# A transformer-like kernel on one core: layer-norm outputs of eleven token tiles transposed by VectorE and DMAs through DRAM in place of TensorE

## Chip, core and metric

The kernel runs on one core of one Trainium2 chip. The metric is the device time of one execution in microseconds. Before the change the median of three runs is 756.94 us (755.6 to 759.04).

## What is computed

Two layers, each a linear-attention block and an expert-lookup block, on 2048 tokens of 576 numbers, all float32:

```python
x = x + A(layernorm(x));  x = x + B(layernorm(x));  x = x + A(layernorm(x));  x = x + B(layernorm(x))

def A(x):                                   # H = 32 heads of 18
    q, k, v = heads(x @ wqkv)
    pq, pk = phi(q), phi(k)                 # phi(t) = where(t > 0, t + 1, exp(t)) + 1e-6
    kv = einsum("bhsd,bhse->bhde", pk, v);  z = einsum("bhsd->bhd", pk)
    o = einsum("bhqd,bhde->bhqe", pq, kv) / (einsum("bhqd,bhd->bhq", pq, z)[..., None] + 1e-6)
    return merged(o) @ wo
```

B scores every token against two sets of eight keys per head, takes the best pair, and adds a gated row of `v` for it. The change lies in the first A block alone.

## The kernel before

The 2048 tokens are cut into 16 tiles of 128. In the first layer, for each tile t, the layer-norm output `y` (128 tokens on the partitions, 576 features along the row, stored as 640 with 64 features doubled) must be turned so that features lie on the partitions; it is then the stationary side of the products with `wqkv`. To keep float32 accuracy a product is made of three passes: each operand is held as a rounded part `hi` and a rest `lo`, so `product` (L205) issues 28 matmuls for one 128 x 576 result.

One tile's way through the first layer's front:

- `first_load` (L587) loads the x tile. `first_ln` (L592): `statistics` (L156) on VectorE (two `BN_STATS`, one `BN_AGGR`, "stf", "mvf") and GpSimd ("rsf"), then `normalized` (L183) on ScalarE writes `y` ("yf", L187).
- `front_T` (L231) calls `transposed` (L190): five TensorE transposes into a PSUM tile "ptf" (L197), then `split` (L100): ScalarE copies to "thif" (L102), VectorE subtracts to "tlof" (L103).
- `front_k` (L234), `front_v` (L239), `front_q` (L250): the products "ppk", "ppv", "ppq" (L212). `phi` (L216) of k and q is one Exp on ScalarE (L218) and two VectorE passes (L219, L221; "ek", "eq"). phi of q goes to DRAM ("pq_d", L254).
- `front_state` (L275): five matmuls add the tile's part of kv into the PSUM tile "kva".

The loop at L724 runs t = 2 to 12. Round t computes k, v, q and the state of tile t, and the layer norm and transposes of tile t + 1. In between it also prepares the second block's weights: while t is at most 9 a round loads eight pieces of `wq_t` ("fold", L540, 288 KB each) and multiplies them at its end (`fold_mm`, L542, "fold_ps"); rounds 4, 6, 8 and 10 also move a finished chunk out (`fold_out`, L553, three ScalarE copies "foldf") and transpose it (`fold_T`, L561: five TensorE transposes "fold_pt", then copies and subtractions "shi" and "slo").

Within a round TensorE runs k, v, q, the transposes of tile t + 1, the state, the fold matmuls. In rounds 10 to 12 the transposes stand ahead of q. The block is inside `in_order` (L142), which ties TensorE, ScalarE, VectorE and GpSimd to the order in which the code issues. SP, which issues all DMAs, isn't tied; its order is the scheduler's, and a DMA that waits on SP holds up those behind it. PSUM has four tiles in rotation: one is "kva" throughout, one "fold_ps" while it fills; the rest serve k, v, q and the transposes. Behind the loop, a long order written out by hand (L752) starts with k and q of tile 13.

Of the kernel before, what the change touches and what calls it, by code (L numbers as in the profile page):

```python
# [11 lines left out]
F32 = mybir.dt.float32  # L12
F32R = mybir.dt.float32r
BF16 = mybir.dt.bfloat16
I32 = mybir.dt.int32
AF = mybir.ActivationFunctionType
ALU = mybir.AluOpType
# [5 lines left out]
P = 128  # L23
NT = S // P
# [11 lines left out]
NB = 5  # L36
# [21 lines left out]
def network(ctx, tc, x_in, wqkv, wo, wq_t, k_t, u_t, v2, c_mask, c_mask4, c_ident, c_code, c_code1, c_scale, c_shift, out):  # L58
    nc = tc.nc

    cp = ctx.enter_context(tc.tile_pool(name="cp", bufs=1))
    wk = ctx.enter_context(tc.tile_pool(name="wk", bufs=2))
    ps = ctx.enter_context(tc.tile_pool(name="ps", bufs=4, space=PSUM))
    dr = ctx.enter_context(tc.tile_pool(name="dr", bufs=1, space=DRAM))

    def psum(name):
        return ps.tile([P, 1024], F32, tag="ps", name=name)
# [28 lines left out]
    hl_d = [dr.tile([P, 2, NB, P], F32, name=f"hl_d{t}") for t in range(NT)]  # L96
    pq_d = [[dr.tile([P, D], F32, name=f"pq_d{l}_{t}") for t in range(NT)] for l in range(2)]
    x_d = [dr.tile([P, D], F32, name=f"x_d{t}") for t in range(NT)]

    def split(src, hi, lo, eng=nc.vector):  # L100

        nc.scalar.activation(hi, src, AF.Copy)  # L102
        eng.tensor_tensor(lo, src, hi.bitcast(F32), op=ALU.subtract)  # L103
# [29 lines left out]
    def split_weight(tiles, c0, hi, lo, rem, which=range(NB), eng=nc.vector):  # L133
        for b in which:
            cols = slice(c0, c0 + D)
            if b != rem:
                split(tiles[b], hi[:, b, cols], lo[:, blocks(rem)[b][1], cols], eng)
            else:
                split_mixed(tiles[b], hi[:, b, cols])

    @contextmanager
    def in_order(*engines):  # L142

        ins = nc.cur_bb.bb.instructions
        last = ins[-1]
        yield
        ins = nc.cur_bb.bb.instructions
        start = next(i for i in reversed(range(len(ins))) if ins[i] is last) + 1
        for e in engines:
            mine = [i for i in ins[start:] if i.engine == e]  # L150
            for x, y in zip(mine, mine[1:]):
                tc.add_manual_dep(y, x.name, mybir.DependencyInfo(mybir.DependencyClass.NoSync, mybir.DependencyReason.DATA),
                                  reason="in_order")
# [28 lines left out]

    def normalized(xt, rs, n):  # L183

        y = wk.tile([P, 2, 320], F32, tag="y", name=f"y{n}", bufs=3)
        x2 = bass.AP(tensor=xt.tensor, offset=xt.offset, ap=[xt.ap[0], [256, 2], [1, 320]])
        nc.scalar.activation(y, x2, AF.Identity, scale=rs[:, 0:1], bias=rs[:, 1:2])  # L187
        return y.rearrange("p a b -> p (a b)")

    def transposed(y, n, more=None, tag="t", step=P):  # L190

        todo = [y[:, b * step:b * step + P] for b in range(NB)] if y is not None else []
        todo += [] if more is None else [more]
        w = len(todo) * P
        pt = psum(f"pt{n}")
        for b, x in enumerate(todo):
            nc.tensor.transpose(pt[:, b * P:(b + 1) * P], x, ident)  # L197
        nb = NB if tag == "t" else NB + 1
        hi = wk.tile([P, nb, P], F32R, tag=tag + "hi", name=f"thi{n}", bufs=4 if tag == "t" else 1)
        lo = wk.tile([P, nb, P], F32R, tag=tag + "lo", name=f"tlo{n}", bufs=4 if tag == "t" else 1)  # L200
        yield
        split(pt[:, :w], hi.rearrange("p a b -> p (a b)")[:, :w], lo.rearrange("p a b -> p (a b)")[:, :w])
        return hi, lo

    def product(tt, hi, lo, cols, n, cut=HALF, rem=REM, by_block=False):  # L205
# [18 lines left out]
    tt = {}  # L224
    xs = {}
    ys = {}
# [3 lines left out]

    def front_T(l, t):  # L231
        tt["f", l, t] = yield from transposed(ys.pop(("f", l, t)), f"f{l}_{t}")

    def front_k(l, t):  # L234
        k = product(tt["f", l, t], whi, wlo, D, f"k{l}_{t}", by_block=(l == 0 and t == 0))
        yield
        tt["fk", l, t] = phi(k, f"k{l}_{t}")
# [175 lines left out]
    def exp_T(l, t, c):  # L413

        y = ys.pop(("b", l, t)) if ok(t) else None
        cg = tt.pop(("cg", l, c)).rearrange("p a b -> p (a b)") if ok(c) else None
        if y is None and cg is None:
            return
        hi, lo = yield from transposed(y, f"b{l}_{t % 99}", cg, tag="t" if cg is None else "u")
        if y is not None:  # L420
            tt["b", l, t] = hi, lo
        if cg is not None:
            b = 0 if y is None else NB
            tt["c", l, c] = hi[:, b], lo[:, b]
# [127 lines left out]

    def fold_out(ch):  # L553
        p = fold_ps.pop(ch)
        f = wk.tile([P, 640], F32, tag="y", name=f"foldf{ch}", bufs=3)
        nc.scalar.activation(f[:, :320], p[:, :320], AF.Copy)
        nc.scalar.activation(f[:, 320:384], p[:, 256:320], AF.Copy)
        nc.scalar.activation(f[:, 384:], p[:, 512:768], AF.Copy)
        fold_st["f", ch] = f
# [21 lines left out]
    def warm_up(n):  # L581

        p = psum("warm")
        for i in range(n):
            nc.tensor.matmul(p[:, :512], junk[:, :P], junk[:, :512], start=True, stop=True)

    def first_load(l, t):  # L587
        xt = wk.tile([P, D], F32, tag="x", name=f"xf_{t}", bufs=3)
        nc.sync.dma_start(xt, x_in[t * P:(t + 1) * P, :])
        xs["f", t] = xt  # L590

    def first_ln(l, t):  # L592
        xt = xs.pop(("f", t))
        ys["f", 0, t] = normalized(xt, statistics(xt, f"f0_{t}"), f"f0_{t}")
# [43 lines left out]
    def ok(t):  # L638
        return 0 <= t < NT
# [3 lines left out]
    def run(l, *seq):  # L643


        for f, t, *n in seq:
            if f is bc or ok(t):
                g = begun.pop((f, l, t), None) or (exp_T(l, *t) if f is bc else f(l, t))
                for i in range(n[0] if n else 99):
                    if g is None or next(g, bc) is bc:  # L650
                        break
                else:
                    begun[f, l, t] = g
# [4 lines left out]
    k, v, q, fT, st = front_k, front_v, front_q, front_T, front_state  # L658
# [3 lines left out]
    L = NT - 1  # L662
# [30 lines left out]
    with in_order(*ALL):  # L693
        x0, x1 = xs.pop(("f", 0)), xs.pop(("f", 1))
        warm_up(14)
        rs0 = statistics(x0, "f0_0", soon=True)
        split_weight(wk_in, D, whi, wlo, REM, (0,))
        ys["f", 0, 0] = normalized(x0, rs0, "f0_0")
        split_weight(wk_in, D, whi, wlo, REM, (1, 2))
        run(0, (fT, 0, 1))  # L700
        warm_up(2)
        run(0, (fT, 0))
        split_weight(wk_in, D, whi, wlo, REM, (3,), nc.gpsimd)
        rs1 = statistics(x1, "f0_1", soon=True)
        split_weight(wk_in, D, whi, wlo, REM, (4,))
        ys["f", 0, 1] = normalized(x1, rs1, "f0_1")
        run(0, (k, 0, 1), (fT, 1))
        split_weight(wv_in, 2 * D, whi, wlo, REM, (0, 1))
        run(0, (k, 0), (k, 1, 1))
        split_weight(wv_in, 2 * D, whi, wlo, REM, (2, 3, 4))  # L710
        first_load(0, 2)
        wq_in = load_weight(wqkv, 0, REM, "w")
        small_loads()
        first_load(0, 3)
        run(0, (k, 1), (v, 0, 1))
        split_weight(wq_in, 0, whi, wlo, REM, (0, 1))
        run(0, (v, 0))
        first_ln(0, 2)
        split_weight(wq_in, 0, whi, wlo, REM, (2, 3))
        run(0, (v, 1, 1))  # L720
        split_weight(wq_in, 0, whi, wlo, REM, (4,))
        run(0, (st, 0), (fT, 2), (v, 1), (q, 0), (st, 1), (q, 1))
        PER, FIRST = 8, 13
        for t in range(2, FIRST):  # L724
            m0 = PER * (t - 2)
            groups = [m for m in range(m0, m0 + PER) if m < 2 * H]
            done = (m0 - 1) // 16 if m0 % 16 == 0 and 0 < m0 <= 2 * H else None
            for m in groups:
                fold_load(m)
            if t + 2 < NT:  # L730
                first_load(0, t + 2)
            if t + 1 < NT:
                first_ln(0, t + 1)
            run(0, (k, t, 1))
            if done is not None:
                fold_out(done)
            run(0, (k, t))
            run(0, (v, t, 1))
            if done is not None and groups:
                fold_T(done)  # L740
            run(0, (v, t))
            if groups:
                run(0, (q, t), (fT, t + 1), (st, t))
            elif t < L:
                run(0, (fT, t + 1), (q if t < L - 1 else st, t), (st if t < L - 1 else q, t if t < L - 1 else -1))
            if done is not None and not groups:
                fold_T(done)
            for m in groups:
                fold_mm(m)
# [101 lines left out]
```

## Time and profile before

| | us |
|---|---|
| median of three runs | 756.94 |
| lowest and highest | 755.6, 759.04 |
| span of the profiled execution (first to last instruction) | 753.7 |
| TensorE busy in it | 736.8 |
| VectorE busy | 456.8 |
| ScalarE busy | 289.1 |

The profiled execution is one run. The profiler gives its span; what lies around the span isn't in the trace, and the median stands 3.2 us above it. A timeline row reads: start, duration of the group, engine, line, operation, output <- inputs, shape, count, and in square brackets how long the engine stood idle before it and what ended that. Rows of consecutive equal instructions are merged. PE is TensorE's matmuls, PEld its weight loads, DVE VectorE, ACT ScalarE, POOL GpSimd, SPq the queue that issues DMAs. Matmuls are pipelined, so a group's duration reaches a little into the next one; the distance between two starts is the better measure.

### The profile page before, as it was taken

The page shows a single profiled execution, that of the slowest core. Times are in us where ns is not written, and L with a number is a line of the kernel's source. Part 1 is how long each engine was busy: PE and PEld are TensorE (multiplying, and loading weights), DVE is VectorE, ACT ScalarE, POOL GpSimd, SP SyncE. Part 2 cuts the span into 40 slices and gives each one's busy share as a digit, 9 for nine tenths or more (in the row PEclk, how much of TensorE's full clock was granted, in tenths as well). Part 3 has the DMA queues.
Part 4 walks back from the last instruction along what each step waited for, and adds up shares of the span by engine and source line. Part 5 has one row for each costly group of instructions (what it writes and reads, how often), then busy time and mean ns, then how long its engine had stood idle before and what let it go on. Part 6 is the DMA issues. An engine that isn't in the chain of part 4 may idle for free.

```text
span 753.7 us, 13987 instructions
## 1 busy us (share of the span) xinstructions
PE 736.8 (98%) x5356; PEld 693.2 (92%) x5356; DVE 456.8 (61%) x1008; ACT 289.1 (38%) x586; POOL 197.7 (26%) x540
## 2 busy tenths in 40 slices
PE   7999999999999999999999999999999999999996
PEld 5999989999998989999999999999999999999984
DVE  5532342324246887666666665563366789999996
ACT  5422232232333544444444443533234333343443
POOL 2110001000002543333333342230033343534331
PEclk9999999999999999999999999999999999999999
DMA  9736446631111322222232211321733213111201
GB/s 275 245 125 223 157 171 220 218 118 49 48 63 32 110 89 77 98 84 83 92 105 101 83 67 60 111 68 38 206 107 112 85 65 115 48 48 58 70 33 63
DMA packets 52267, 79.48 MB, mean 105 GB/s; under 512 B 5480, under 2 KB 22376, under 8 KB 52200
## 3 DMA queue, kind: packets, MB, share of 16 engines
q1 hardware_dynamic: 52200, 78.59, 31.8%
q8 instruction: 42, 0.69, 0.4%
q14 instruction: 25, 0.20, 0.1%
HBM read 55.01 MB, written 23.56 MB: 104 GB/s over the span
## 4 chain that ended last, share of the span: by engine, by line
PE 81%; DVE 10%; ACT 3%; issue 2%; POOL 2%; DMA 1%; SPq 0%; DVEq 0%; POOLq 0%; ACTq 0%
PE ppk L212 15%; PE ppv L212 15%; PE ppo L402 13%; PE pps L433 12%; PE ppq L212 11%; PE kva L283 4%; PE fold_ps L550 2%; PE ptf L197 2%; PE ptb L197 2%; PE po L517 2%; PE pto L197 2%; PE m L332 1%; DVE tloo L103 1%; DVE o L379 1%; DVE x L391 1%
## 5 line engine op out<-in xcount | busy, mean ns | idle before, releaser
L219 DVE TENSOR_SCALAR ek<-ek 128x576 f32<-128x576 f32 x32 | 14.7, 459 | 81.4 <-ACT ek L218 76.9
L212 PE MATMUL ppk<-whi,thif 128*128 128x288 f32 x320 | 50.4, 301 | 1.6 <-ACT thif L102 1.6
L402 PE MATMUL ppo<-ohi,thio 126*128 126x288 f32 (+1 forms) x320 | 50.9, 301 | 0.8 <-DVE ct L492 0.5
L212 PEld LDWEIGHTS ppk<-whi,thif 128*128 128x128 f32 x320 | 44.2, 188 | 5.6 <-issue 3.3
L163 POOL TENSOR_SCALAR rsf<-mvf 128x1 f32<-128x1 f32 x16 | 3.1, 192 | 175.6 <-DVE mvf L161 175.4
L212 PE MATMUL ppk<-whi,tlof 128*128 128x288 f32 x320 | 48.7, 296 | 0.3 <-DVE tlof L103 0.3
L212 PE MATMUL ppv<-whi,thif 128*128 128x252 f32 x320 | 48.0, 296 | 0.1
L187 ACT ACTIVATE yb<-x,rsb 128x640 f32<-128x640 f32 x32 | 29.5, 923 | 47.9 <-POOL rsb L180 47.9
L212 PE MATMUL ppv<-whi,tlof 128*128 128x252 f32 x320 | 47.6, 295 | 0.0
L219 DVE TENSOR_SCALAR eq<-eq 128x576 f32<-128x576 f32 x32 | 15.8, 493 | 51.7 <-ACT eq L218 51.7
L433 PE MATMUL pps<-shi,thib 128*128 128x512 f32 x160 | 44.4, 407 | 2.0 <-ACT thib L102 2.0
L402 PEld LDWEIGHTS ppo<-ohi,thio 126*128 126x128 f32 (+1 forms) x320 | 44.6, 189 | 1.9 <-issue 0.7
L212 PEld LDWEIGHTS ppk<-whi,tlof 128*128 128x128 f32 x320 | 44.6, 188 | 0.5 <-DVE tlof L103 0.5
L212 PEld LDWEIGHTS ppv<-whi,tlof 128*128 128x128 f32 x320 | 44.6, 188 | 0.0
L212 PEld LDWEIGHTS ppv<-whi,thif 128*128 128x128 f32 x320 | 44.2, 188 | 0.3 <-ACT thif L102 0.3
L438 ACT ACTIVATE s<-pps 128x512 f32<-128x512 f32 x32 | 19.1, 596 | 61.4 <-PE pps L433 61.4
L433 PE MATMUL pps<-shi,tlob 128*128 128x512 f32 x160 | 42.5, 395 | 0.0
L103 DVE TENSOR_TENSOR tlof<-ptf,thif 128x640 fp32r<-128x640 f32 x32 | 26.2, 818 | 24.3 <-ACT thif L102 24.2
L402 PE MATMUL ppo<-ohi,tloo 126*128 126x288 f32 x256 | 40.3, 295 | 0.0
L402 PE MATMUL ppo<-olo,thio 126*128 126x288 f32 x256 | 40.3, 296 | 0.0
L212 PE MATMUL ppk<-wlo,thif 128*128 128x288 f32 x256 | 39.9, 296 | 0.0
L212 PE MATMUL ppq<-whi 128*128 128x288 f32 x260 | 39.6, 299 | 0.1
(156 smaller groups left out, 1778.6 us busy)
## 6 DMA issues: line engine op xcount, KB each, us to landing
fold<-in_wq_t SPq DMA_DIRECT2D x64, 288.0 KB, 4.8
whi<-hl_d SPq DMA_DIRECT2D x26, 320.0 KB, 3.5
pq_d<-eq SPq DMA_DIRECT2D x19, 288.0 KB
pq<-pq_d SPq DMA_DIRECT2D x19, 288.0 KB, 3.3
xf<-in_x SPq DMA_DIRECT2D x16, 288.0 KB, 4.7
x<-in_x SPq DMA_DIRECT2D x16, 288.0 KB, 2.8
x_d<-x SPq DMA_DIRECT2D x16, 288.0 KB, 3.1
x<-x_d SPq DMA_DIRECT2D x16, 288.0 KB, 2.6
```

The source lines that it names most:

```text
L103: eng.tensor_tensor(lo, src, hi.bitcast(F32), op=ALU.subtract)
L187: nc.scalar.activation(y, x2, AF.Identity, scale=rs[:, 0:1], bias=rs[:, 1:2])
L197: nc.tensor.transpose(pt[:, b * P:(b + 1) * P], x, ident)
L212: nc.tensor.matmul(o[:, at:at + c1 - c0], tt[a == "lo"][:, b, :], wb[:, cols + c0:cols + c1], start=(i == 0), stop=(i == len(todo) - 1))
L219: nc.vector.tensor_scalar(e, e, 1.0, EPS, op0=ALU.min, op1=ALU.add)
L283: nc.tensor.matmul(a[:w, c * HC:(c + 1) * HC], vt[:, c * w:(c + 1) * w], fk[:, c * HC:(c + 1) * HC], start=(t == 0 and c == 0), stop=(t == ...
L332: nc.tensor.matmul(m[:c, h * 512:h * 512 + HALF], kvb[:n, b * HC:b * HC + c], wob[l][b][:n, h * HALF:(h + 1) * HALF], start=True, stop=True)
L402: nc.tensor.matmul(p[:, h * 512:h * 512 + HALF], hl[a][:r, b], w[:r, h * HALF:(h + 1) * HALF], start=(i == 0), stop=(i == len(todo) - 1))
L433: nc.tensor.matmul(p[:, :512], hl[a == "lo"][:, b, :], shi[:, b] if w == "hi" else slo[:, blocks(REM)[b][1]], start=(i == 0), stop=(i == l ...
L438: nc.scalar.activation(s[:, NE:], p[:, :512], AF.Copy)
L517: nc.tensor.matmul(p[:, b * 512:b * 512 + HALF], c[i], vmix[:, b * HALF:(b + 1) * HALF], start=(i == 0 and not based), stop=(i == 1))
L550: nc.tensor.matmul(p[32 * j:32 * j + 32, at:at + c1 - c0], kpad[:, ch // 2, 24 - 8 * a:56 - 8 * a], st[:, c0:c1], start=(a == 0), stop=(a ...
```

## The change

In rounds 2 to 12, so for tiles 3 to 13, the transposes leave TensorE. `front_flip` for tile t + 1 stands behind phi of `k(t)`: VectorE transposes the 32 x 32 blocks of `y` within each group of 32 partitions (one instruction, output `q`), one DMA writes `q` (128 x 640, 320 KB) to a DRAM tile `t_d`, and four DMAs, 80 KB each in pieces of 160 numbers (640 bytes), bring it back into a tile `r`, so that each block lands on its right partitions. `front_flipped` takes the place of the transposes' copies: ScalarE copies `r` to "thif", VectorE subtracts to "tlof", now from SBUF and in runs of 32. The tag "y" grows from three buffers to four, since `q` and `r` share it. Rounds 10 to 12 keep their order (tile t + 1 ahead of q). Tiles 0 to 2, 14 and 15 and all later transposes stay on TensorE.

```diff
+    t_d = [dr.tile([P, NB * P], F32, name=f"t_d{t}") for t in range(NT)]
...
-        y = wk.tile([P, 2, 320], F32, tag="y", name=f"y{n}", bufs=3)
+        y = wk.tile([P, 2, 320], F32, tag="y", name=f"y{n}", bufs=4)
...
+    def flip(y, d, n):
+
+        q = wk.tile([P, NB * P], F32, tag="y", name=f"q{n}", bufs=4)
+        nc.vector.transpose(q.rearrange("p (q b c) -> p b q c", q=4, b=NB), y.rearrange("p (b q c) -> p b q c", b=NB, q=4))
+        nc.sync.dma_start(d, q)
+        r = wk.tile([P, NB * P], F32, tag="y", name=f"r{n}", bufs=4)
+        w = 32 * NB
+        for a in range(4):
+            nc.sync.dma_start(r[32 * a:32 * a + 32].rearrange("r (i e) -> r i e", i=4),
+                              d[:, a * w:(a + 1) * w].rearrange("(i r) e -> r i e", i=4))
+        return r
+
+    def flipped(r, n):
+
+        hi = wk.tile([P, NB, P], F32R, tag="thi", name=f"thi{n}", bufs=4)
+        lo = wk.tile([P, NB, P], F32R, tag="tlo", name=f"tlo{n}", bufs=4)
+        src = r.rearrange("p (i b c) -> p b i c", i=4, b=NB)
+        h, l = (x.rearrange("p b (i c) -> p b i c", i=4) for x in (hi, lo))
+        nc.scalar.activation(h, src, AF.Copy)
+        nc.vector.tensor_tensor(l, src, h.bitcast(F32), op=ALU.subtract)
+        return hi, lo
...
+    def front_flip(l, t):
+        ys["r", l, t] = flip(ys.pop(("f", l, t)), t_d[t], f"f{l}_{t}")
+
+    def front_flipped(l, t):
+        tt["f", l, t] = flipped(ys.pop(("r", l, t)), f"f{l}_{t}")
...
             run(0, (k, t))
+            front_flip(0, t + 1)
             run(0, (v, t, 1))
...
             if groups:
-                run(0, (q, t), (fT, t + 1), (st, t))
+                run(0, (q, t), (front_flipped, t + 1), (st, t))
             elif t < L:
-                run(0, (fT, t + 1), (q if t < L - 1 else st, t), (st if t < L - 1 else q, t if t < L - 1 else -1))
+                run(0, (front_flipped, t + 1), (q, t), (st, t))
```

SP's DMAs in round 3, before, from the x load on ("xf" x tile, "pq_d" the store of phi of q, "fold" the next round's weight pieces; the number behind a name's underscore is the tile's):

```order
L589 DMA xf_1042<-in_x 128x576
L254 DMA pq_d_3_106<-eq_3_810 128x576
L540 DMA fold_850<-in_wq_t 128x576
L540 DMA fold_852<-in_wq_t 128x576
L540 DMA fold_854<-in_wq_t 128x576
```

And SP at the same place now ("t_d" is the DRAM tile, "qf" the flipped tile, "rf" the tile read back, x4 the four reads):

```order
L210 DMA t_d_155<-qf_4_767 128x640
L618 DMA xf_1064<-in_x 128x576
L214 DMA rf_4_770<-t_d_155 32x4x160 x4
L283 DMA pq_d_3_106<-eq_3_836 128x576
L569 DMA fold_870<-in_wq_t 128x576
```

The write of tile 4 stands ahead of an x load, and the four reads, which wait for the write, ahead of the store of phi of q and the next eight fold loads.

VectorE in rounds 3 to 4, before ("stf" and "mvf" are the statistics of tile 5):

```order
L221 SCALAR_TENSOR_TENSOR ek_3_745<-ppk_3_716,ek_3_745 128x576
L219 TENSOR_SCALAR eq_3_810<-eq_3_810 128x576
L221 SCALAR_TENSOR_TENSOR eq_3_810<-ppq_3_781,eq_3_810 128x576
L103 TENSOR_TENSOR tlof_4_822<-ptf_4_815,thif_4_821 128x640
L158 BN_STATS stf_5_864<-xf_703 128x6
```

And VectorE at the same place now:

```order
L244 SCALAR_TENSOR_TENSOR ek_3_763<-ppk_3_734,ek_3_763 128x576
L209 STREAM_TRANSPOSE qf_4_767<-yf_4_732 128x5x4x32
L242 TENSOR_SCALAR eq_3_836<-eq_3_836 128x576
L244 SCALAR_TENSOR_TENSOR eq_3_836<-ppq_3_807,eq_3_836 128x576
L225 TENSOR_TENSOR tlof_4_842<-rf_4_770,thif_4_841 128x640
L159 BN_STATS stf_5_884<-xf_721 128x6
```

The flip of tile 4 stands behind phi of k of tile 3; the statistics of tile 5 still stand behind "tlof" of tile 4, which now comes from the tile read back.

ScalarE from round 10 into round 12, before ("ek" and "eq" are the Exp of k and q, "v" the copies of v):

```order
L102 ACTIVATE thif_11_1951<-ptf_11_1945 128x640
L218 ACTIVATE eq_10_1984<-ppq_10_1955 128x576
L572 ACTIVATE shi<-fold_pt_1994 128x4x4x7 x5
L187 ACTIVATE yf_12_2021<-xf_1863,rsf_12_2017 128x640
L218 ACTIVATE ek_11_2052<-ppk_11_2023 128x576
L245 ACTIVATE v_1_86<-ppv_11_2056 128x2x126 x2
L248 ACTIVATE v_1_86<-ppv_11_2056 128x72
L102 ACTIVATE thif_12_2094<-ptf_12_2088 128x640
L218 ACTIVATE eq_11_2127<-ppq_11_2098 128x576
L187 ACTIVATE yf_13_2148<-xf_2010,rsf_13_2144 128x640
L187 ACTIVATE yf_14_2331<-xf_2137,rsf_14_2327 128x640
L218 ACTIVATE ek_12_2179<-ppk_12_2150 128x576
```

And ScalarE at the same place now:

```order
L224 ACTIVATE thif_11_1985<-rf_11_1948 128x640
L241 ACTIVATE eq_10_2018<-ppq_10_1989 128x576
L601 ACTIVATE shi<-fold_pt_2028 128x4x4x7 x5
L188 ACTIVATE yf_12_2055<-xf_1895,rsf_12_2051 128x640
L241 ACTIVATE ek_11_2086<-ppk_11_2057 128x576
L274 ACTIVATE v_1_86<-ppv_11_2098 128x2x126 x2
L277 ACTIVATE v_1_86<-ppv_11_2098 128x72
L224 ACTIVATE thif_12_2130<-rf_12_2093 128x640
L241 ACTIVATE eq_11_2163<-ppq_11_2134 128x576
L188 ACTIVATE yf_13_2184<-xf_2044,rsf_13_2180 128x640
L241 ACTIVATE ek_12_2215<-ppk_12_2186 128x576
L188 ACTIVATE yf_14_2369<-xf_2173,rsf_14_2365 128x640
```

The copy "thif" stands where it stood, ahead of q's Exp, but reads "rf", which arrives by DMA; "yf" of tile 14 has moved behind the Exp of k of tile 12.

More of the change, by code (lines that the diff above doesn't have):

```diff
@@ L554, in fold_out @@
         p = fold_ps.pop(ch)
-        f = wk.tile([P, 640], F32, tag="y", name=f"foldf{ch}", bufs=3)
+        f = wk.tile([P, 640], F32, tag="y", name=f"foldf{ch}", bufs=4)
         nc.scalar.activation(f[:, :320], p[:, :320], AF.Copy)
```

## The prediction

> **What bounds the kernel now.** I read the page's header first, then the busy times per stretch for the rounds of the loop that the change touches (each stretch runs from the first matmul of one `k` product to that of the next), then the timeline inside those rounds, and last the list of DMAs with their times to landing.
>
> ```profile
> span 753.7 us, 13987 instructions
> PE 736.8 (98%) x5356; PEld 693.2 (92%) x5356; DVE 456.8 (61%) x1008; ACT 289.1 (38%) x586; POOL 197.7 (26%) x540
> ```
>
> ```profile
> 36.92:51.86 14.94, 14.94 (x134) 13.84 (x132) 6.05 (x13) 4.13 (x8) 1.01 (x3) 1.00 0.17 58
> 51.86:66.90 15.04, 15.04 (x136) 13.94 (x132) 4.10 (x9) 3.60 (x7) 1.01 (x3) 1.00 0.57 198
> 66.90:82.49 15.59, 15.59 (x140) 14.49 (x137) 5.75 (x13) 5.33 (x15) 1.01 (x3) 1.00 0.55 191
> 158.80:172.10 13.30, 13.30 (x109) 13.30 (x105) 2.74 (x6) 4.31 (x10) 1.01 (x3) 1.00 0.40 126
> 172.10:185.38 13.28, 13.03 (x102) 12.79 (x100) 5.42 (x13) 4.69 (x12) 1.01 (x3) 1.00 0.14 47
> 185.38:198.16 12.78, 12.78 (x103) 12.78 (x101) 5.00 (x12) 4.40 (x8) 2.02 (x6) 1.00 0.23 70
> ```
>
> The rows are rounds t = 2, 3, 4, 10, 11 and 12; the columns are length, then PE, PEld, DVE, ACT and POOL busy, granted clock, DMA share, GB/s. TensorE fills every round; the other engines stand about half idle. So each microsecond that TensorE loses, or is made to wait, in this stretch is a microsecond of the end. Rounds 5, 7, 9 are built like 3, and 6, 8 like 4 (which also transposes a folded weight chunk).
>
> **What it removes.** Five TensorE transposes per tile. Their price is the distance from their start to the next group's:
>
> ```profile
> 63.13 0.71 PE L197 MATMUL ptf<-ident,yf 128*128 128x128 f32 x5
> 63.68 1.05 PE L283 MATMUL kva<-ek,v 128*127 128x126 f32 x8
> ```
>
> 0.55 us a tile, 11 tiles: 6.05 us is the whole prize. One fewer PSUM slot is taken too; nothing but 0.25 us in round 11 waits on one (13.28 against 13.03 busy), so I cost that at nothing.
>
> **What it adds: a round trip with a deadline.** Tile t+1 is flipped on VectorE right behind phi of `k(t)`, written to DRAM, read back by four DMAs, copied by ScalarE (`thif`), and only then can `k(t+1)` begin. Call D the time from the start of `k(t)` to the end of phi, and N the time from there to the first matmul of `k(t+1)`. The next round starts at D + N, or when TensorE is done, whichever is later.
>
> D comes from the timeline. Rounds 2 and 3:
>
> ```profile
> 43.95 0.76 DVE L221 SCALAR_TENSOR_TENSOR ek<-ppk,ek 128x576 f32<-128x576 f32 x1 [0.52 <-DVE ek L219]
> 50.22 0.81 DVE L103 TENSOR_TENSOR tlof<-ptf,thif 128x640 fp32r<-128x640 f32 x1
> 53.45 0.92 ACT L187 ACTIVATE yf<-xf,rsf 128x640 f32<-128x640 f32 x1 [3.91 <-POOL rsf L166]
> 55.90 0.65 ACT L218 ACTIVATE ek<-ppk 128x576 f32<-128x576 f32 x1 [1.52 <-PE ppk L212]
> 57.15 0.76 DVE L221 SCALAR_TENSOR_TENSOR ek<-ppk,ek 128x576 f32<-128x576 f32 x1
> 63.88 0.70 ACT L102 ACTIVATE thif<-ptf 128x640 fp32r<-128x640 f32 x1
> ```
>
> Round 2: 43.95 + 0.76 - 36.92 = 7.79. Round 3: 57.15 + 0.76 - 51.86 = 6.05.
>
> N, step by step, from these rows (VectorE's quickest pass of this kind, then DMAs with KB each and time to landing, then issues on SP):
>
> ```profile
> L219 DVE TENSOR_SCALAR ek<-ek 128x576 f32<-128x576 f32 x32 | 14.7, 459 | 81.4 <-ACT ek L218 76.9
> ```
>
> ```profile
> fold<-in_wq_t SPq DMA_DIRECT2D x64, 288.0 KB, 4.8
> whi<-hl_d SPq DMA_DIRECT2D x26, 320.0 KB, 3.5
> x<-x_d SPq DMA_DIRECT2D x16, 288.0 KB, 2.6
> out<-x SPq DMA_DIRECT2D x16, 288.0 KB, 2.1
> hl_d<-thif SPq DMA_DIRECT2D x13, 320.0 KB, 2.6
> hl_d<-tlof SPq DMA_DIRECT2D x13, 320.0 KB, 3.2
> ```
>
> ```profile
> 525.80 0.38 SPq L266 DMA_DIRECT2D whi<-hl_d  x1
> 526.22 0.53 SPq L267 DMA_DIRECT2D whi<-hl_d  x1
> ...
> 527.36 0.52 SPq L267 DMA_DIRECT2D whi<-hl_d  x1
> ```
>
> - The flip: no such instruction is in the trace. Nearest is `tlof`, VectorE over 128x640 f32, 0.81. Bounds: 0.51 (the quicker 128x576 pass of L219, its row above, scaled to 640) and 1.6 (twice `tlof`).
> - The write of 320 KB: 2.6 as `hl_d<-thif`, the same size and way; bounds 2.1 (`out<-x`) and 3.2 (`hl_d<-tlof`).
> - Issuing the reads: the four issues from 525.80 to 527.36 stand 0.52 apart; three spacings are 1.56. Lower bound 1.26 (three of its shortest, 0.42).
> - The last read: 2.6 as `x<-x_d`; it is smaller (80 KB) but in pieces. Bounds 2.1 and 3.5 (`whi<-hl_d`).
> - The `thif` copy: 0.70, and an estimated 0.2 for the hand-overs.
>
> N = 0.81 + 2.6 + 1.56 + 2.6 + 0.70 + 0.2 = 8.5; all low ends together make 6.9, all high ends about 10.9. [...]
>
> Does other traffic stretch N? The fold loads fill the DMA engines for the first half of a round:
>
> ```profile
> 58.00:59.00 1.00, 1.00 (x10) 1.00 (x10) 0.00 (x0) 0.00 (x0) 0.00 (x0) 1.00 1.05 406
> 60.00:61.00 1.00, 1.00 (x9) 1.00 (x8) 0.00 (x0) 0.44 (x3) 0.00 (x0) 1.00 0.06 17
> ```
>
> They drain about 8 us into round 3 (51.86); the flip's write is issued at about 6.9, now ahead of the x load on SP, so it queues behind little. What stands behind SP's new wait for the write (the `pq_d` store, the next fold loads) comes later anyway, at phi of `q`. I add nothing.
>
> **Late copies delay the next flip.** If `thif` is what a round waits for, `tlof` and the next tile's statistics start that late too. Before, `tlof` start to `yf` end took 53.45 + 0.92 - 50.22 = 4.15; starting at the round's begin it ends at 4.1, against 4.04 (55.90 - 51.86) when ScalarE's Exp wants to run: D becomes 6.15. In rounds with fold copies these stand between:
>
> ```profile
> 160.39 0.92 ACT L187 ACTIVATE yf<-xf,rsf 128x640 f32<-128x640 f32 x1 [3.91 <-POOL rsf L166]
> 161.64 0.38 ACT L558 ACTIVATE foldf<-fold_ps 128x256 f32<-128x256 f32 x1
> ```
>
> They end 0.71 after `yf`: Exp at 4.85, D = 6.86.
>
> Rounds 10 to 12 have no fold matmuls left to hide anything, and there `thif` stands ahead of `q`'s Exp on ScalarE, so phi of `q` and all VectorE work behind it slips:
>
> ```profile
> 173.62 0.63 DVE L576 TENSOR_TENSOR slo<-fold_pt,shi 128x112 fp32r<-128x112 f32 x2 [0.79 <-ACT shi L572]
> ...
> 179.76 0.76 DVE L221 SCALAR_TENSOR_TENSOR ek<-ppk,ek 128x576 f32<-128x576 f32 x1
> ...
> 185.86 0.76 DVE L221 SCALAR_TENSOR_TENSOR eq<-ppq,eq 128x576 f32<-128x576 f32 x1
> ...
> 189.19 0.92 ACT L187 ACTIVATE yf<-xf,rsf 128x640 f32<-128x640 f32 x1 [3.94 <-POOL rsf L166]
> ...
> 190.47 0.92 ACT L187 ACTIVATE yf<-xf,rsf 128x640 f32<-128x640 f32 x1 [0.35 <-POOL rsf L166]
> ...
> 191.30 0.63 ACT L218 ACTIVATE ek<-ppk 128x576 f32<-128x576 f32 x1
> ...
> 192.52 0.76 DVE L221 SCALAR_TENSOR_TENSOR ek<-ppk,ek 128x576 f32<-128x576 f32 x1
> ```
>
> Round 11: before, D = 179.76 + 0.76 - 172.10 = 8.42, with `slo` at 1.52 into the round. Now VectorE runs `tlof` 0.81, then phi of `q` 0.46 + 0.76, so `slo` begins at about 2.0: D = 8.9. Round 12: before, 192.52 + 0.76 - 185.38 = 7.90; phi of `q` ends 0.8 later than its 1.24 (185.86 + 0.76 - 185.38), but the order puts the second `yf` behind Exp, which saved 191.30 - (189.19 + 0.92) = 1.2: D = 7.5.
>
> **The sum**, new length less old:
> - round 2: 7.79 + 8.5 - 14.94 = +1.35
> - rounds 3, 5, 7, 9: 6.15 + 8.5 = 14.65 less 15.04 = -0.39 each, -1.56
> - rounds 4, 6, 8: 6.86 + 8.5 = 15.36 less 15.59 = -0.23 each, -0.69
> - round 10: 15.36 less 13.30 = +2.06
> - round 11: 8.9 + 8.5 - 13.28 = +4.12
> - round 12: 7.5 + 8.5 - 12.78 = +3.22
>
> Together +8.5 us on the span of 753.7. The median, 756.94, lies 3.2 above that span; I put the difference on it: 765.4. Half of one per cent, 3.8 us, is about what a measurement of this kernel can tell from no change (its three runs lie within 3.4). Behind round 12 nothing gives it back: TensorE stays the full engine (98% above), and the stage behind the loop starts from the sums that the loop ends with.
>
> **The rivals.**
>
> *The trip is short and hidden: faster.* If N were 6 or less, rounds 2 to 10 would all be TensorE-bound at -0.55 each, -5 us, and only rounds 11 and 12 would pay (+1.6, +0.7): about -2.6; with N near 5 round 11 would pay 0.6 and round 12 gain 0.3, -4.6, 752.3. For it: 61% VectorE, idle DMA late in each round. Against it: two DMAs in a row alone take 4.2 at the lowest row, plus the issue of four. It needs N under 5.4, where the low ends of every row make 6.9. The sum changes sign at N = 7.0; N from 5.4 to 7.8 is "no change" (within 3.8).
>
> *TensorE's clock falls in the new gaps: slower still.* Before, the granted clock is 0.9 or more in all 40 slices, and TensorE's waits are short, 0.81 as early as the first product:
>
> ```profile
> PEclk9999999999999999999999999999999999999999
> ```
>
> ```profile
> 9.55 0.53 PE L212 MATMUL ppk<-whi,thif 128*128 128x288 f32 x2 [0.81 <-ACT thif L102]
> ```
>
> In my sum TensorE stands idle some 2.6, 4.7 and 3.8 us before `k(11)`, `k(12)`, `k(13)` (round length less its own work, 13.30, 13.28 and 12.78 less 0.55). If the clock halved, a `k` product (28 of round 11's 102 recorded matmuls, so about 28/102 of 13.03 = 3.6 us) would take twice as long behind one or two of those gaps: +3.6 to +7.2 more, 769 to 773. [...]
>
> *The reads crawl or collide.* At N = 9.5 every round from 2 on is late by itself, since rounds 3 to 9 have only 0.4 us to spare: +19.5 us, 776. For it: `fold` loads land in 4.8 under traffic, pieces are 640 bytes. Against: the engines are at 0.06 by then.
>
> **How the numbers follow.** Forecast (late at rounds 2 and 10 to 12, full clock) 0.51; clock falls 0.17; long trip 0.11; no change 0.14; faster 0.07. The first three are slower: 0.79. The range runs from N = 7.0 (757) to N = 9.5 (about 777), which takes in the clock case and leaves out faster, a bit of no change and the longest trips.
>
> **What would show it.** After: `thif` in rounds 10 to 12 ending its idle time on a DMA and `k(11)` to `k(13)` waiting on `thif` by 2.6, 4.7 and 3.8 us; rounds 3 to 9 a little shorter than before; round 2 about 16.3. Wrong if `k(12)` starts without a wait, if rounds 3 to 9 lengthen (N over 8.9), or if the clock column leaves 1.00.

## The result: 0.6% slower, and the profile after

The changed kernel takes 761.99 us (median of 10 runs, 759.29 to 763.72) against 757.04 for the kernel before (10 runs, 755.48 to 759.04): a ratio of 1.0062, with a 95% interval from 1.0046 to 1.0078. The forecast was slower, at 765.4. The late round trip that it describes is there; the price is smaller, and part of it arises where the forecast put nothing.

The page of the changed kernel:

```profile
span 759.7 us, 13977 instructions
...
PE 733.8 (97%) x5301; PEld 689.7 (91%) x5301; DVE 467.3 (62%) x1019; ACT 289.5 (38%) x586; POOL 196.5 (26%) x540
```

TensorE has less to do (733.8 us after 736.8) in a span that is 6.0 us longer. Where it stands idle, the busy times per stretch show. The changed kernel's rounds 2, 3, 4, 5, 7, 10, 11 and 12, each from the first matmul of one `k` product to that of the next (columns as in the prediction):

```profile
37.81:52.90 15.09, 14.46 (x128) 13.29 (x127) 5.36 (x11) 4.27 (x8) 1.00 (x3) 1.00 0.33 103
52.90:67.39 14.49, 14.49 (x127) 13.39 (x127) 5.44 (x10) 3.62 (x7) 1.00 (x3) 1.00 0.72 235
67.39:82.42 15.03, 15.03 (x135) 13.93 (x131) 6.37 (x15) 5.36 (x15) 1.00 (x3) 1.00 0.72 241
82.42:97.39 14.97, 14.56 (x130) 13.38 (x126) 4.69 (x10) 3.74 (x7) 1.00 (x3) 1.00 0.76 254
112.43:128.39 15.96, 14.56 (x130) 13.39 (x126) 4.24 (x10) 3.74 (x7) 1.01 (x3) 1.00 0.74 249
158.19:172.21 14.02, 12.98 (x99) 12.75 (x100) 3.73 (x8) 3.73 (x10) 1.00 (x3) 1.00 0.58 187
172.21:188.38 16.17, 12.44 (x95) 12.29 (x95) 6.42 (x15) 4.61 (x13) 1.00 (x3) 1.00 0.26 79
188.38:203.10 14.72, 13.95 (x94) 13.81 (x94) 5.64 (x13) 4.43 (x9) 2.01 (x6) 0.88 0.35 105
```

In rounds 3 and 4 length equals PE's busy time: TensorE bounds them still, and they are 0.55 shorter. In rounds 5 and 7, built like 3, the same work (14.56) stands in 14.97 and 15.96. Rounds 10 to 12 are all longer than before. New length less old, with rounds 6, 8 and 9 (15.04, 15.04, 14.76) beside those shown: round 2 +0.15; 3, 5, 7, 9 -0.55, -0.07, +0.92, -0.28; 4, 6, 8 -0.56, -0.55, -0.56; 10 to 12 +0.72, +2.89, +1.94. The sum is +4.05.

Who is late, the waits between 36 and 215 us say (engine and line, what it waited for, us in total, times, longest):

```profile
ACT thif L224 <- DMA rf<-t_d: 28.6, 11, 6.9
...
PE ppk L235 <- ACT thif L224: 8.2, 7, 3.7
```

ScalarE waits for the read-back in all eleven rounds, TensorE for ScalarE's copy in seven. One trip in a quiet stretch, round 11, in the timeline (`ek` is phi of k, `qf` the flip, `t_d` the write, `rf` the four reads):

```profile
180.31 0.76 DVE L244 SCALAR_TENSOR_TENSOR ek<-ppk,ek 128x576 f32<-128x576 f32 x1
180.98 0.83 DVE L209 STREAM_TRANSPOSE qf<-yf 128x640 f32<-128x640 f32 x1
181.84 0.32 SPq L210 DMA_DIRECT2D t_d<-qf  x1
184.15 1.74 SPq L214 DMA_DIRECT2D rf<-t_d  x4
187.59 0.74 ACT L224 ACTIVATE thif<-rf 128x640 fp32r<-128x640 f32 x1 [6.87 <-DMA rf<-t_d]
...
188.38 2.26 PE L235 MATMUL ppk<-whi,thif 128*128 128x288 f32 x10 [3.73 <-ACT thif L224]
190.43 2.12 PE L235 MATMUL ppk<-wlo,thif 128*128 128x288 f32 x8
```

Phi ends at 180.31 + 0.76 = 181.07 and `k(12)` starts at 188.38: N = 7.31. Its parts: to the write's issue 0.77 (the flip), from there to the first read's issue 2.31, three spacings of reads 1.74 x 3/4 = 1.3, from the last read's issue to `thif` 2.1, and `thif` to the matmul 0.79. Rounds 2, 10 and 12, worked out alike, give 7.30, 7.26 and 7.16.

The same trip in round 7:

```profile
117.72 0.76 DVE L244 SCALAR_TENSOR_TENSOR ek<-ppk,ek 128x576 f32<-128x576 f32 x1
...
119.26 0.33 SPq L210 DMA_DIRECT2D t_d<-qf  x1
...
123.87 1.75 SPq L214 DMA_DIRECT2D rf<-t_d  x4
...
128.39 0.40 PE L235 MATMUL ppk<-whi,thif 128*128 128x288 f32 x1 [1.40 <-ACT thif L224]
```

The write takes 123.87 - 119.26 = 4.61 where round 11's took 2.31, and N is 128.39 - 118.48 = 9.91. What else the DMA engines do during these two writes (length, five engines' busy time, clock, DMA share, GB/s):

```profile
119.26:123.87 4.61, 4.61 (x37) 4.61 (x36) 0.00 (x0) 0.78 (x3) 0.00 (x0) 1.00 0.78 296
181.84:184.15 2.31, 2.31 (x21) 2.31 (x20) 0.00 (x0) 0.00 (x0) 0.00 (x0) 1.00 0.36 142
```

296 GB/s against 142: in round 11 next to nothing moves but the write's own 320 KB, in round 7 fold loads move beside it. Over all eleven rounds the write takes longer the more else moves: 2.16 to 2.31 us with at most 0.09 MB of other data, 2.42 with 0.28, 2.90 with 0.59, 3.79 with 0.95, 4.61 with 1.04 (GB/s times length, less the write). That fits a write that shares the engines with the fold loads; a longer write also lets more pass, so it is no proof.

### The profile page after: what moved, and what is told of

Its sections match the earlier page's. It is cut to its first block, busy times and chain, and to the rows that moved or that the text cites. A ratio compares the mean times of both kernels' runs of the same rounds, so it can differ in the third digit from the quotient of the medians.

```text
span 759.7 us, 13977 instructions
## 1 busy us (share of the span) xinstructions
PE 733.8 (97%) x5301; PEld 689.7 (91%) x5301; DVE 467.3 (62%) x1019; ACT 289.5 (38%) x586; POOL 196.5 (26%) x540
## 4 chain that ended last, share of the span: by engine, by line
PE 71%; DVE 13%; DMA 5%; ACT 4%; issue 3%; POOL 2%; SPq 2%; DVEq 0%; ACTq 0%; POOLq 0%
PE ppk L235 14%; PE ppo L431 12%; PE ppv L235 12%; PE pps L462 11%; PE ppq L235 9%; PE kva L312 3%; DMA t_d<-qf 3%; PE ptb L198 2%; DMA rf<-t_d 2%; PE po L546 2%; PE pto L198 2%; PE ptf L198 1%; PE m L361 1%; PE fold_ps L579 1%; SPq L214 1%
## 5 line engine op out<-in xcount | busy, mean ns | idle before, releaser
L104 DVE TENSOR_TENSOR tlob<-ptb,thib 128x768 fp32r<-128x768 f32 (+2 forms) x37 | 31.2, 844 | 14.0 <-ACT thib L103 13.8
```

## The experiments

The theory (A): the round trip is about 7.3 us when the DMA engines are quiet and up to 9.9 under fold traffic; it is hidden in rounds 3, 4, 6 and 8, and late in 2, 5, 7, 9 and 10 to 12. The rivals: flipping itself, or its traffic, costs wherever it is done (B); the write waits in SP's queue; the clock's fall in the gaps is what the last rounds pay. Edits are given against the changed kernel. The kernels of the first four and of the last four runs each share their runs of the kernel before, with medians of 756.3 and 756.68 us.

**Only the fold rounds.** Tiles 3 to 10 take the trip, 11 to 13 go back to TensorE.

```diff
-            front_flip(0, t + 1)
+            if groups:
+                front_flip(0, t + 1)
...
-                run(0, (front_flipped, t + 1), (q, t), (st, t))
+                run(0, (fT, t + 1), (q, t), (st, t))
```

> Only tiles 3 to 10 take the way through DRAM (rounds 2 to 9, with fold matmuls behind q); tiles 11 to 13 are transposed on TensorE as before. Theory A, a round trip with a deadline: the rounds behave as in the profile after, where rounds 2 to 9 together are 1.5 us shorter than before (+0.15, -0.55, -0.56, -0.07, -0.55, +0.92, -0.55, -0.28), and rounds 10 to 12 fall back to 13.3, 13.3 and 12.8; so about 1.5 us faster than before, 755.5, within what can be told from no change. Theory B, a cost per tile (the added VectorE pass, five more DMAs, SP's time) that does not depend on the round: 8 of 11 tiles, so 8/11 of the measured +4.95, about +3.6 us, 760.6.

Median 754.30 us, ratio 0.9994 (0.9975 to 1.0013). Rounds 7 and 11:

```profile
112.36:126.99 14.63, 14.56 (x126) 13.39 (x126) 4.95 (x10) 3.62 (x7) 1.00 (x3) 1.00 0.76 248
...
169.82:183.11 13.29, 13.06 (x103) 12.82 (x101) 5.44 (x13) 4.68 (x12) 1.00 (x3) 1.00 0.15 46
```

Rounds 10 to 12 are back at before's lengths, and the loop is 3.2 us shorter than before in the profiled execution. That is near theory A's 755.5 and far from B's 760.6: the loss lies in the last rounds, and the trip alone doesn't make a round slow. The ratio's interval takes in no change: eight of the eleven executions lie between 752.8 and 756.4 and three between 758.4 and 760.6. In those three the mean granted clock is 0.994 or 0.995, in the others 0.996 to 0.998, so TensorE's clock fell for longer in them; what set that off is open.

**Only the last rounds.** Tiles 11 to 13 take the trip, 3 to 10 stay on TensorE.

```diff
-            front_flip(0, t + 1)
+            if not groups:
+                front_flip(0, t + 1)
...
-                run(0, (q, t), (front_flipped, t + 1), (st, t))
+                run(0, (q, t), (fT, t + 1), (st, t))
```

> The other part alone: only tiles 11 to 13 take the way through DRAM (rounds 10 to 12, which have no fold matmuls); tiles 3 to 10 are transposed on TensorE. Theory A: rounds 10 to 12 cost what they cost in the profile after, +0.7, +2.9 and +1.9, so +5.5 us on before, 762.5, slower than the whole change. Theory B: 3 of 11 tiles, +1.35 us, 758.4.

Median 762.43 us, ratio 1.0082 (1.0069 to 1.0095), as theory A says: the whole loss, from three tiles. Rounds 11 and 12, then two groups of `k(12)` and the Exp behind it:

```profile
173.25:189.44 16.19, 12.45 (x94) 12.31 (x94) 6.40 (x15) 4.60 (x13) 1.00 (x3) 0.96 0.25 78
189.44:205.07 15.63, 14.87 (x94) 14.72 (x94) 5.65 (x13) 4.43 (x9) 2.01 (x6) 0.83 0.34 100
```

```profile
189.44 2.77 PE L235 MATMUL ppk<-whi,thif 128*128 128x288 f32 x10 [3.74 <-ACT thif L224]
192.01 2.12 PE L235 MATMUL ppk<-wlo,thif 128*128 128x288 f32 x8
...
195.90 0.65 ACT L241 ACTIVATE ek<-ppk 128x576 f32<-128x576 f32 x1 [0.92 <-PE ppk L235]
```

Round 11 is +2.91, as in the changed kernel. Round 12 is 0.91 longer than there, and ScalarE's Exp waits 0.92 for the slow product: here the clock's fall costs. Round 10 is only +0.25, where +0.7 was expected, so the sum came out at 762.4 partly by two misses that cancel.

**No trip.** The copies read VectorE's output directly; the five DMAs are left out.

```diff
-        nc.sync.dma_start(d, q)
-        r = wk.tile([P, NB * P], F32, tag="y", name=f"r{n}", bufs=4)
-        w = 32 * NB
-        for a in range(4):
-            nc.sync.dma_start(r[32 * a:32 * a + 32].rearrange("r (i e) -> r i e", i=4),
-                              d[:, a * w:(a + 1) * w].rearrange("(i r) e -> r i e", i=4))
-        return r
+        return q
```

> As after, but without the five DMAs of each tile: the flipped tile is copied straight from VectorE's output, so that blocks stand on the wrong partitions (the eleven tiles' products are computed from wrongly placed numbers; everything else is as after). VectorE's transpose, the copies from SBUF and the missing TensorE work stay. Theory A: only the trip costs, so every round is bound by TensorE and shrinks by 0.55: -5.5 to -6.0 us on before, 751. Theory B: the added VectorE pass and the changed copies carry a cost of their own, so it stays within 2 us of before, 755 or more.

Median 750.27 us, ratio 0.9926 (0.9914 to 0.9938). Rounds 3 and 11:

```profile
51.91:66.40 14.49, 14.49 (x131) 13.39 (x127) 4.86 (x10) 3.62 (x7) 1.00 (x3) 1.00 0.59 206
...
167.74:179.96 12.22, 12.22 (x97) 12.22 (x96) 6.21 (x14) 4.83 (x12) 1.00 (x3) 1.00 0.17 51
```

Every round is bound by TensorE, and all are about 0.55 shorter than before but round 11, which is 1.06 shorter. The loop gains 6.6. With TensorE filling every round, the flip and the strided copies cost nothing; the loss comes with the five DMAs of the trip.

**The flip ahead of phi.** `front_flip` moves from behind `k(t)` to right behind the layer norm.

```diff
             if t + 1 < NT:
                 first_ln(0, t + 1)
+            front_flip(0, t + 1)
...
             run(0, (k, t))
-            front_flip(0, t + 1)
```

> As after, but the flip stands right behind the layer norm of its tile, ahead of phi of k, so that the trip starts about 3.5 us earlier in most rounds (yf ends about 2.5 into a round where nothing is late, phi of k at 6.05). Theory A: the deadline is met in all rounds but 11 (there yf itself is late, 6.5 into the round, and 6.5 + 7.3 = 13.8 against 13.3 before): 10 times -0.55 and +0.5, about -5 us, 752. The write now queues behind the fold loads on the DMA engines; if that costs more than the 3.5 us gained, rounds 3 to 9 are late as before. Theory B: no change against after, 762.

Median 756.35 us, ratio 1.0002 (0.9991 to 1.0013): the loss is gone, but not the 4 us more that I expected. Rounds 2 to 9 come as expected but one (round 8, 15.39). Rounds 11 and 12 don't:

```profile
168.21:183.44 15.23, 12.45 (x94) 12.30 (x94) 6.39 (x15) 4.61 (x13) 1.01 (x3) 1.00 0.27 83
183.44:198.53 15.09, 13.92 (x95) 13.78 (x95) 5.63 (x13) 4.41 (x9) 2.02 (x6) 0.89 0.35 103
```

```profile
189.01 0.35 SPq L383 DMA_DIRECT2D x<-in_x  x1
189.02 0.84 DVE L209 STREAM_TRANSPOSE qf<-yf 128x640 f32<-128x640 f32 x1 [1.71 <-ACT yf L188]
...
189.89 0.32 SPq L210 DMA_DIRECT2D t_d<-qf  x1
194.25 1.74 SPq L214 DMA_DIRECT2D rf<-t_d  x4
```

The flip waits for `yf`, so the write of round 12 leaves 189.89 - 183.44 = 6.45 into the round instead of 196.72 - 188.38 = 8.34, and then takes 4.36 instead of 2.16. An x load has been issued 0.88 ahead of it, but that alone doesn't set the time, for in round 11 an x load stands as far ahead and the write takes 3.02:

```profile
175.20 0.35 SPq L618 DMA_DIRECT2D xf<-in_x  x1
...
176.09 0.32 SPq L210 DMA_DIRECT2D t_d<-qf  x1
...
179.11 1.74 SPq L214 DMA_DIRECT2D rf<-t_d  x4
```

Why these two differ is open. In round 11 layer norm itself is late (`yf` ends 6.96 into the round), so moving the flip within the round wins little; in round 12 `yf` ends 5.54 into it, and most of what is lost is the longer write.

**The write on ScalarE's queue.**

```diff
-        nc.sync.dma_start(d, q)
+        nc.scalar.dma_start(d, q)
```

> As after, but the flip's write is issued by ScalarE's queue in place of SP's. In the profile after the write takes 2.2 us from its issue to the reads' issue in rounds without fold loads (2, 10 to 12), and 2.3 to 4.6 in rounds 3 to 9. Theory A, the write waits in line behind fold loads on the same queue: from another queue it takes about 2.2 to 2.5 everywhere, rounds 5, 7 and 9 become TensorE-bound, 2.2 us less than after, about 759.8. Theory B, it shares the DMA engines with whatever moves and the queue doesn't matter: 2.3 to 4.6 as before and 762.

Median 767.77 us, ratio 1.0139 (1.0108 to 1.0171). Rounds 7, 8 and 10, and the write and reads of round 7:

```profile
112.99:130.43 17.44, 14.56 (x131) 13.40 (x127) 4.75 (x10) 3.74 (x7) 1.01 (x3) 0.99 0.69 232
130.43:146.85 16.42, 16.42 (x131) 15.32 (x132) 7.56 (x16) 5.37 (x15) 1.01 (x3) 0.90 0.56 196
...
164.98:181.03 16.05, 15.70 (x99) 15.46 (x99) 3.73 (x8) 3.85 (x10) 1.01 (x3) 0.81 0.42 141
```

```profile
119.82 0.33 ACTq L210 DMA_DIRECT2D t_d<-qf  x1
125.08 1.75 SPq L214 DMA_DIRECT2D rf<-t_d  x4
```

Neither theory's time came. The write takes 5.26 in round 7, for 4.61 in the changed kernel, and 2.16 in round 8, for 2.31. N, from the end of phi to the next `k` product, is 130.43 - 119.04 = 11.39 in round 7 and 164.98 - 152.90 = 12.08 in round 9, for 9.91 and 8.71; in rounds 10 to 12 it is 7.29, 7.29 and 7.11, for 7.26, 7.31 and 7.16. From another queue the write wasn't shorter, so standing behind others in SP's queue was not the cause. Why it got worse is open. Round 8 is of use by itself: TensorE fills it, has round 6's work and takes 16.42 instead of 15.04, with the granted clock at 0.90 behind a wait of 2.88 us. That is 1.38 us for one fall of the clock. Round 10, behind a wait of 3.57, has the clock at 0.81: phi of k ends 8.76 into it instead of 6.76, and it takes 16.05 instead of 14.02.

**TensorE kept busy.** 4, 16 and 8 spare bfloat16 matmuls behind the state's in rounds 10, 11 and 12.

```diff
+        WARM = {10: 4, 11: 16, 12: 8}
...
+                warm_up(WARM[t])
```

> As after, with spare TensorE matmuls (4, 16 and 8 of 128x512 bf16 on a tile of zeros) behind the state of rounds 10, 11 and 12, so that TensorE doesn't stand idle before the next k product. In the profile after, the k product of tile 12 starts behind a gap of 3.7 us and takes about 5.3 us in place of 3.9: the clock fell. Theory A: that costs nothing, because phi of k of tile 12 waits for the layer norm of tile 13 on ScalarE until the same moment, and the next deadline is the round trip: no change against after, 762. Theory B, the fallen clock is part of the loss: 1.4 us less than after, 760.6, and the k product of tile 12 at 3.9.

Median 760.86 us, ratio 1.0051 (1.0033 to 1.0069), an interval that overlaps with the changed kernel's. Round 12:

```profile
188.98:203.47 14.49, 14.12 (x102) 12.96 (x103) 5.65 (x13) 4.32 (x9) 2.02 (x6) 1.00 0.36 106
```

The clock stays at 1.00, and the round is 0.23 shorter than in the changed kernel. Round 11 stays at 16.28, so with the clock up the trip is as late as before. What the fall costs the median there, about 1 us or less, can't be told from nothing by this run.

**Fold rounds only, with the early flip.** The edits of the first and the fourth experiment together.

```diff
+            if groups:
+                front_flip(0, t + 1)
             run(0, (k, t))
-            front_flip(0, t + 1)
...
-                run(0, (front_flipped, t + 1), (q, t), (st, t))
+                run(0, (fT, t + 1), (q, t), (st, t))
```

> Tiles 3 to 10 only, with the early flip of the fourth experiment; tiles 11 to 13 on TensorE. Theory A: rounds 2 to 9 all TensorE-bound at -0.55 (as they are in the fourth experiment, but for one at -0.2), rounds 10 to 12 as before: -4.0 to -4.4 us on before, 752. Theory B, moving the flip only shifts the loss to later rounds: no change from before, 756.

Median 752.89 us, ratio 0.9949 (0.9933 to 0.9966). Round 7:

```profile
110.87:125.36 14.49, 14.49 (x130) 13.39 (x126) 4.37 (x9) 3.74 (x7) 1.01 (x3) 1.00 0.81 250
```

Rounds 2 to 9 are all at TensorE's own length; the loop is 4.4 us shorter than before, which is eight tiles at 0.55.

**Two rounds ahead.** All eleven tiles, with layer norm and flip of tile t + 2 in round t.

```diff
-            if t + 1 < NT:
-                first_ln(0, t + 1)
+            for u in ([t + 1] if t == 2 else []) + ([t + 2] if t + 2 < 14 else []):
+                first_ln(0, u)
+                front_flip(0, u)
...
-            front_flip(0, t + 1)
```

> All eleven tiles, with layer norm and flip two rounds ahead of use (round t prepares tile t + 2; round 2 prepares tiles 3 and 4), the copy still at the end of the round before use. The trip then has more than a round of about 12 us. Theory A: no product waits for it; all eleven rounds shrink by 0.55 as in the run without the trip, less up to 1 us in round 2, where two flips stand ahead of phi of k: -5 to -6 us on before, 751. Theory B, traffic and queues set the loss: 754 or more.

Median 750.53 us, ratio 0.9924 (0.9908 to 0.9939): faster than both kernels. Rounds 2, 3 and 11:

```profile
36.86:52.07 15.21, 14.62 (x128) 13.31 (x127) 8.80 (x18) 5.08 (x9) 2.02 (x6) 1.00 0.43 132
52.07:66.56 14.49, 14.49 (x131) 13.39 (x127) 4.33 (x8) 3.63 (x7) 1.01 (x3) 1.00 0.81 245
...
167.90:180.12 12.22, 12.22 (x97) 12.22 (x96) 6.94 (x17) 5.53 (x13) 2.02 (x6) 1.00 0.24 80
```

All the same DMAs run, under fold traffic too (0.81 of the engines in round 3), and no round but the second waits. Round 2, with two flips ahead of phi, is 0.82 over its 14.39 in the run without the trip. With enough lead the trip itself costs nothing.

## Why the prediction was right, and where its sizes were off

**The prize, 0.55 us a tile: right.** The run without the trip gains it in every round. The PSUM wait of round 11, costed at nothing, was worth another 0.5 there.

**D: right.** Forecast for rounds 2, 3, 11 and 12: 7.79, 6.15, 8.9, 7.5; measured (start of `k` to end of phi) 7.79, 6.04, 8.86, 7.56. Only the rounds with fold copies came earlier, 6.27 to 6.76 for 6.86. So the indirect effects (late `tlof`, late statistics, phi of `q` behind `thif`) were rightly placed.

**N: the mis-sized term.** 8.5 was forecast; in quiet rounds it is 7.2 to 7.3. Of the difference, the write is 0.3 (2.31 for 2.6), the reads' issue 0.25 (1.3 for 1.56), the last read 0.5 (2.1 for 2.6), flip and hand-overs 0.15 (no row stood behind the 0.2 for hand-overs; in round 11 they take 0.03, from 181.81 to 181.84, and 0.05, from 188.33 to 188.38). The rows came from transfers in other stretches of the kernel; why each is a little longer than here isn't shown. With N shorter by about 1.2, rounds 2 and 10 to 12 cost 5.05 less than forecast, and rounds 4, 6 and 8 another 0.98, since they hid the trip altogether.

**"Does other traffic stretch N? ... I add nothing": wrong.** The prediction went by what stands in SP's queue, and by engines drained 8 us into the round; the write leaves at 119.26 - 112.43 = 6.83, before that, and takes 2.3 to 4.6 us in rounds 3 to 9. N was 8.92, 9.91 and 8.71 in rounds 5, 7 and 9, so rounds 3, 5, 7 and 9 together came out at +0.02 where -1.56 was forecast. The rival of the long trip was thus right for three rounds, by way of the write and not of the reads. The size of this term isn't steady: rounds 3, 5, 7 and 9, built alike, come to -1.73 in the first experiment's profiled execution and to +0.62 in the sixth's.

**The sum.** Forecast +8.5, measured +4.05 in the loop: 5.05 and 0.98 too much, 1.58 too little. The profiled span grew by 6.0. The rest of that, 0.89 ahead of round 2 and 1.06 behind the loop, I don't put on the change: over the ten kernels profiled the loop's start scatters between 36.86 and 37.87, and the stretch behind it between 555.5 and 556.9, longest in the run without the trip. Each execution takes 1.7 to 2.1 us more than its own span, so the medians stand 3.2 and 2.3 above the spans because both profiled executions were faster than their medians; the 0.9 between them is the last of the 3.4 us that the forecast was over.

**The short trip** fell: N never was under 7.1, where 5.4 was needed. But the direction owes something to luck. With the measured N of 7.3 the forecast's own sum gives +2.1 us, which is inside its "no change" (3.8 us, N from 5.4 to 7.8). What brought the loop to +4.05 instead is rounds 5, 7 and 9, together 2.2 us longer than TensorE's own work, through the traffic that was costed at nothing: an N too long and a traffic term too short partly cancelled. (The sum changes sign at N = 6.8; at the 7.0 given it is still +0.9.)

**The signs** came out mixed. `k(11)`, `k(12)` and `k(13)` all waited on `thif`, by 1.03, 3.73 and 0.77 where 2.6, 4.7 and 3.8 were forecast; before `k(13)` the slowed product had taken up part of the gap (TensorE is busy 13.95 in round 12, against 12.22 in the run without the trip). Two of the three signs of being wrong appeared: round 7 lengthened, with N at 9.91 (the other rounds from 3 to 9 shrank), and the clock column left 1.00 in round 12.

**The clock** fell once in these rounds, behind the 3.73 us wait for `k(12)` (0.88 in round 12; `k(12)`'s first two groups take 2.26 and 2.12, in round 11's product 1.59 and 1.23). It cost next to nothing in this execution, because the Exp behind it was held by layer norm until the same moment:

```profile
192.99 0.92 ACT L188 ACTIVATE yf<-xf,rsf 128x640 f32<-128x640 f32 x1 [4.12 <-POOL rsf L167]
193.93 0.65 ACT L241 ACTIVATE ek<-ppk 128x576 f32<-128x576 f32 x1
```

`yf` ends at 193.91, Exp starts at 193.93. In the experiments such a fall did cost, 0.9, 1.38 and 2.0 us, less than the 3.6 to 7.2 of the rival: of the changed kernel's three gaps only the one of 3.73 us had a fall behind it, and the clock came back after 3.4 or 6.8 us. The rival's halved clock behind one or two of the gaps was the author's assumption: no run had shown it in these rounds, and in the changed kernel the clock was 0.50 behind one of the three, for 3.4 us. The changed kernel's clock also fell once ahead of the rounds, some 8 us into the span, behind a wait of 1.98 us (0.56, 0.50, 0.50 and 0.73 in the four microseconds from 8 on). Waits of 2.78 us (the early flip, ahead of `k(12)`) and 2.88 us (the write on ScalarE's queue, ahead of `k(8)`) had a fall behind them too (0.89 and 0.90 in the rounds they begin); waits of 1.40 us (the changed kernel, ahead of `k(8)`) and 1.62 us (TensorE kept busy, ahead of `k(6)`) had none (1.00 in both rounds).

## What to carry to other kernels

A piece of work moved off the full engine saves what it took there only if its new path is shorter than the time between its input and its deadline: measure that time in each kind of round, and if the path is longer, give it a round more of lead. For a path through DMAs, take the price from a quiet stretch and then again under the traffic that runs where it will stand, in more than one execution. The first experiment to make is the one without the path: here it showed that moving the transposes is worth 0.7% (ratio 0.9926) and that the loss comes with the trip; the run two rounds ahead then showed that it is the trip's timing.

## What the runs showed of the hardware

- A 320 KB write from SBUF to DRAM takes 2.2 to 2.3 us from its issue to the issue of the read that waits for it when little else moves, and up to 4.61 beside fold loads (296 GB/s in all), 5.26 from ScalarE's queue (round 7, 232 GB/s in all), and 6.11 in round 9 of the run with the fold rounds only and the early flip (144.38 to 150.49). With one 288 KB load issued 0.88 or 0.89 us ahead it took 4.36 and 3.02.
- VectorE's transpose of 32 x 32 blocks takes 0.83 us for 128 x 640 float32 in the changed kernel, where the subtraction pass `tlof` over the same size takes 0.825 on average.
- Behind waits of 1.98 and of 2.78 to 3.74 us TensorE's granted clock was 0.50 for 3.4 us (five times, two of them worked out from a round's mean clock) or 6.8 us (twice), then 1.00 at once (each kernel's last 12 us left out); a round that TensorE fills got 1.38 us longer by it. In the second experiment the fall began within the wait (0.54 from 188 to 189, the product at 189.44), in the changed kernel some 0.7 us after TensorE had started again (1.00 from 188 to 189, 0.52 from 189 to 190, the product at 188.38). Equal waits didn't cost the same: 3.73 us in the changed kernel was followed by 3.4 us at 0.50, 3.74 us in the second experiment by 6.8. In the changed kernel, 3 and 5 us after 188.38 (the seventh column is the clock):

```profile
191.00:192.00 1.00, 1.00 (x6) 1.00 (x6) 0.93 (x4) 0.00 (x0) 0.19 (x1) 0.50 0.71 276
...
193.00:194.00 1.00, 1.00 (x10) 1.00 (x8) 0.00 (x0) 0.98 (x2) 0.78 (x3) 1.00 0.00 0
```

Six matmuls run in the first of these microseconds, ten in the second.
